# Scaled queries written once and spread over two head tiles by small transfers

## The chip, the cores and the metric

One core of a Trainium2 chip runs the whole kernel. The metric is the device time of one execution in microseconds (us). The kernel before takes 842.66 us, the median of three runs (841.91 to 842.76).

## The reference

Two independent parts are computed and laid side by side in the output (1 x 2048 x 1024). Part A is multi-head attention over 2048 tokens with 32 heads of 16 features; part B is a long causal convolution.

```
def _A_ref(x, wqkv, wo):                 # x 1x2048x512, H = 32, Dh = 16
    qkv = (x @ wqkv).reshape(B, S, 3, H, Dh) ...
    scores = einsum("bhqd,bhkd->bhqk", q, k) * (Dh ** -0.5)
    p = softmax(scores, axis=-1)
    o = einsum("bhqk,bhkd->bhqd", p, v)
    return o.transpose(...).reshape(B, S, D) @ wo

def _B_ref(q, k, v, shift_k, ssm_k, ssm_D):
    k_shift = four-tap causal filter of k with shift_k
    kv = k_shift * v
    y = causal convolution of kv with ssm_k (2048 taps, by FFT) + kv * ssm_D
    return q * y
```

## The kernel before

**Attention.** The 32 heads stand in four groups ("octets") of eight, so that eight heads of 16 features fill the 128 partitions. The queries stand in four blocks of 512. That gives 16 pairs (octet, query block), numbered p in `PAIRS` (L350), and each pair has two groups n = 2p and 2p+1: four of its eight heads are the even ones, four the odd ones. One group is 16 key tiles of 128 keys by 4 heads, 64 blocks, so there are 32 x 64 = 2048 blocks in all. A block is one matmul of 32 contraction rows (L670): its keys are 32 partitions of `KTo`, holding two neighbouring heads, its queries are 32 partitions of `QT`. So that only one of the two heads counts, the `QT` tile of parity par (0 for even heads, 1 for odd) must be zero in the 16 rows of the other head. `QT` has three slots of two such tiles (`R_Q` = 3), slot p % 3 for pair p.

The score blocks land in PSUM banks 0 to 5. ScalarE (ACT) takes two or three adjacent banks in one exponential (`emit_exp`, L703) and writes them to `PT`. Some blocks are given to VectorE (DVE) instead (`exp_on_dve`, L739 to 763): five DVE instructions per block, one that reads the bank into `FX` (L745), three steps of a polynomial in `EH` (L752) and one that writes `PTD` (L757). TensorE (PE) then multiplies the exponentials by the values (`emit_pv`, L786, bank 6), the DVE divides by the sums (`finish_group`, L847 to 867), and the output projection follows (L897, L905).

**Queries.** A projection unit ("q", p) is four matmuls (L390) into one bank. `evac_unit` (L433) then takes it out in two DVE passes (L440). Each reads the whole bank, multiplies by a column of `MASK` and writes a whole `QT` tile; `MASK` holds the scale in the rows of one parity and 0 in the rows of the other. Pair 0 has passes of its own (L541).

**Convolution.** Rows of the reversed filter are loaded from a scratch in device memory into four slots of `WR`, 128 "quads" of four 512 KB transfers, issued on SP's queue (`load_wr`, L932). They are multiplied on PE in steps of four small matmuls (`conv_lags`, L956, bank 7), 8192 in all.

**Order of work.** Every instruction is recorded by a planner in Python that keeps an estimated clock for each engine (`Eng.op`, `dma`) and fixes the program order of each engine before the program is built; on the chip, the engines wait for each other by semaphores alone. The main loop (L1183) goes over T, one round for each ACT exponential: `emit_qk` gives out banks and score matmuls, `pv_step` the value matmuls, `emit_bg` background work (projection units by their due rounds in `jobs`, L1007, and convolution steps), `warm_up` (L1161) fills PE's remaining time with matmuls of zeros. DVE work is put in place by `urgent` (L287) and `advance` (L277). The constants at the top (L38 to L97) set margins, window lengths and the convolution's pace. POOL's queue carries a few memsets, the loads and stores of `QN`, the load of the output weights and the output stores (L908). A unit ("q", p) is due eight rounds before its pair's first round and can be placed once pair p - 3 has had its last score matmul.

Of the kernel before, what the change touches and what calls it, by code (L numbers as in the profile page):

```python
# [15 lines left out]
QB = 512  # L16
# [20 lines left out]
N_OPEN = 68  # L37
LAGS = 8  # L38
PACE = 1.0
KEYS0 = 256  # L40
# [20 lines left out]
SLOT = 16  # L61
OPEN = 70
CLOSE = 10
REST = 2
LEN = 4
WIN_D = 2
S_U = 0.4
S_FX = 0.45
# [3 lines left out]
JOIN = 0.05  # L72
JOIN2 = 0.1
MOST = 3
LOOK = 8
GAP = 8
# [4 lines left out]
BACKLOG = 5.8  # L81
MARGIN = 0.3
SPARE = 0
# [12 lines left out]
WAIT = 1.5  # L96
LATE = 0.1  # L97
V512 = (0.60, 0.726)
# [68 lines left out]
def bass_concat_heads__mha_block__ssm_conv_h3__prompt_kernel(  # L167
# [21 lines left out]
    def sem(name):  # L189
        return enter(nc.semaphore(name))  # L190

    def sb(name, shape, dt=BF16):
        return enter(nc.sbuf_tensor(name, shape, dt))
# [4 lines left out]
    QT = sb("QT", [128, R_Q, 2, QB])  # L198
    VA = sb("VA", [128, 2, KT, VROW])
    PT = sb("PT", [128, R_PT, QB])  # L200
    WR = sb("WR", [128, R_W, S])
# [93 lines left out]
    d_q = [DmaSem(sem(f"d_q{i}")) for i in range(2)]  # L295
    d_outB = [DmaSem(sem(f"d_outB{i}")) for i in range(2)]
    d_outE = DmaSem(sem("d_outE"))
    d_outA = [DmaSem(sem(f"d_outA{i}")) for i in range(R_A)]
# [45 lines left out]
    pool.op(lambda e: e.memset(VA[:, :, :, 0:8 * VW].rearrange("p s k (h e) -> p (s k) h e", e=VW)[:, :, :, DH:VW], 1.0))  # L344
    h_va1 = pool.op(lambda e: e.memset(VA[:, :, :, 8 * VW:VROW].rearrange("p s k e -> p (s k) e"), 1.0))
    h_kz0 = pool.op(lambda e: e.memset(KZS[:, :, S:S + PAD], 0.0))
    act.op(lambda e: e.activation(JNK[:, 1:2], JNK[:, 0:1], ACT.Exp), [h_j], inc=False)
# [85 lines left out]
    def evac_unit(u, bank, h):  # L433
        kind = u[0]
        if kind == "q":
            p = u[1]
            last = [qk_done[2 * (p - R_Q) + i] for i in range(2)] if p >= R_Q else []
            for par in range(2):
                hh = urgent(
                    lambda e, par=par: e.tensor_scalar(QT[:, p % R_Q, par, :], PS[:, bank, :], MASK[:, par:par + 1], None, ALU.mult),  # L440
                    [h, h_mask] + last, us=(0.658, 0.784))
                h_q[2 * p + par] = hh
        elif kind == "k":
# [560 lines left out]
    def step(n):  # L1004
        return PLAN * n // (NQB * NG)

    jobs = [(step(2 * p) - 8, ("q", p)) for p in range(2, 16)]  # L1007
    jobs += [(step(OF.index(o)) - 16 + 4 * sc, (x, o, sc)) for o in (2, 3) for sc in range(4) for x in "kv"]
# [250 lines left out]
```

## Time and profile before

| | us |
|---|---|
| median of three timed runs | 842.66 (841.91 to 842.76) |
| the profiled execution, its own time | 845.53 |
| its span, first to last instruction | 843.8 |
| ACT busy | 828.5 (98%) |
| DVE busy | 812.1 (96%) |
| PE busy | 788.0 (93%) |
| POOL busy | 17.6 (2%) |

The span is the time from the first to the last instruction of the profiled execution; 1.7 us of its own time lie outside. Matmuls overlap on PE, so its busy share is no measure of how near its peak it runs. In a row of a group, the numbers after the first bar are the time in which at least one instruction of the group ran and the mean duration of one, in nanoseconds; after the second bar stands the idle time of the engine just before them and what ended it. Instructions of ACT and DVE overlap their neighbours at the ends, so that the mean duration is larger than the distance from start to start.

### The profile page before, as it was taken

How to read it: one execution, taken by the hardware profiler on the slowest of the kernel's cores; microseconds unless marked ns; L12 is line 12 of the kernel's file. 1: busy time of each engine (PE TensorE's matmuls, PEld its weight loads, DVE VectorE, ACT ScalarE, POOL GpSimd, SP SyncE). 2: the span in 40 equal slices, each digit the busy share in tenths (PEclk: the TensorE clock that was granted, in tenths of full speed). 3: DMA queues.
4: the chain of work that ended last, by engine and by line, in shares of the span. 5: the costliest groups of instructions: out<-in, count | busy, mean ns of one | idle time of the engine just before them, and what ended most of it. 6: DMA issues, size and time to landing. Idle time of an engine off the chain costs nothing.

```text
span 843.8 us, 30582 instructions
## 1 busy us (share of the span) xinstructions
PE 788.0 (93%) x13766; PEld 334.9 (40%) x13808; DVE 812.1 (96%) x1382; ACT 828.5 (98%) x727; POOL 17.6 (2%) x34
## 2 busy tenths in 40 slices
PE   8898999999999999999999999999999999999897
PEld 3343334443433334344434434344443434343342
DVE  4999999999999999999999999999999999999895
ACT  6999999999999999999999999999999999999897
POOL 2000000000000000000000100000000000010000
PEclk9999999999999999999999999999999999999899
DMA  9996199999999999989999999999999999999942
GB/s 227 262 297 245 48 406 386 359 385 366 395 354 395 350 376 332 348 270 342 404 380 388 384 391 380 369 408 398 405 408 350 378 407 410 403 347 360 354 181 75
DMA packets 105394, 289.44 MB, mean 343 GB/s; under 512 B 35760, under 2 KB 37808, under 8 KB 104880
## 3 DMA queue, kind: packets, MB, share of 16 engines
q1 hardware_dynamic: 102256, 280.80, 90.3%
q0 software_dynamic: 1808, 6.29, 2.2%
q8 instruction: 109, 1.79, 0.8%
q10 hardware_dynamic: 1200, 0.39, 0.2%
q14 instruction: 21, 0.17, 0.1%
HBM read 276.83 MB, written 6.42 MB: 336 GB/s over the span
## 4 chain that ended last, share of the span: by engine, by line
ACT 95%; PE 3%; SPq 1%; DMA 1%; issue 0%; DVE 0%
ACT PT L703 94%; PE PS L670 1%; SPq L257 1%; DMA xT<-in_A_x_dram 1%; PE PS L956 1%; PE PS L786 1%; PE PS L897 0%; DVE DT L847 0%; ACT QT L915 0%; PE PS L1161 0%; DVE FX L745 0%; PE PS L399 0%; PE PS L981 0%; PE PS L422 0%; DVE DTN L858 0%
## 5 line engine op out<-in xcount | busy, mean ns | idle before, releaser
L703 ACT ACTIVATE PT<-PS 128x1536 bf16<-128x1536 f32 (+2 forms) x722 | 825.5, 1455 | 4.1 <-PE PS L670 3.7
L670 PE MATMUL PS<-QT,KTo 32*128 32x512 bf16 x2048 | 285.8, 385 | 34.7 <-ACT PT L703 8.3
L752 DVE SCALAR_TENSOR_TENSOR EH<-EH,FX 128x512 f32<-128x512 f32 x446 | 295.3, 678 | 0.2
L956 PE MATMUL PS<-WR,KV 128*16 128x128 bf16 (+15 forms) x8192 | 218.9, 220 | 2.6 <-issue 2.6
L786 PE MATMUL PS<-PT,VA 128*32 128x512 bf16 x1825 | 197.9, 390 | 2.0 <-DVE DT L847 1.1
L956 PEld LDWEIGHTS PS<-WR,KV 128*14 128x14 bf16 (+15 forms) x8192 | 146.8, 87 | 88.9 <-issue 53.7
L1161 PE MATMUL PS<-IDN,ZW 128*32 128x512 bf16 (+4 forms) x666 | 168.5, 335 | 0.9 <-DVE DT L847 0.6
L670 PEld LDWEIGHTS PS<-QT,KTo 32*128 32x128 bf16 x2048 | 72.5, 91 | 230.9 <-ACT PT L703 180.1
L745 DVE TENSOR_SCALAR FX<-PS 128x512 f32<-128x512 f32 x223 | 151.8, 682 | 5.3 <-PE PS L670 4.5
L752 DVE SCALAR_TENSOR_TENSOR EH<-FX 128x512 f32<-128x512 uint16 x223 | 150.6, 681 | 0.1
L757 DVE SCALAR_TENSOR_TENSOR PTD<-EH,FX 128x512 uint16<-128x512 f32 x223 | 150.3, 676 | 0.1
L786 PEld LDWEIGHTS PS<-PT,VA 128*32 128x32 bf16 x1825 | 47.6, 93 | 108.0 <-issue 95.0
L786 PE MATMUL PS<-PTD,VA 128*32 128x512 bf16 x223 | 69.4, 384 | 0.0
L1161 PEld LDWEIGHTS PS<-IDN,ZW 128*32 128x32 bf16 (+1 forms) x666 | 54.4, 96 | 25.4 <-issue 6.3
L847 DVE STREAM_TRANSPOSE DT<-PS 128x512 f32<-128x512 f32 x32 | 22.7, 709 | 8.4 <-PE PS L786 7.8
L970 DVE CAST YB<-PS 128x512 bf16<-128x512 f32 x32 | 21.8, 681 | 1.0 <-PE PS L956 0.5
L440 DVE TENSOR_SCALAR QT<-PS,MASK 128x512 bf16<-128x512 f32 x30 | 20.9, 737 | 0.6 <-PE PS L390 0.3
L422 PE MATMUL PS<-WKV,xT 128*128 128x128 bf16 x256 | 19.0, 220 | 0.4 <-DVE KTo L446 0.2
L399 PE MATMUL PS<-xT,WKV 128*128 128x512 bf16 (+1 forms) x50 | 15.1, 373 | 3.8 <-issue 1.6
L897 PE MATMUL PS<-WKV,OTN 128*128 128x512 bf16 x51 | 16.4, 383 | 2.2 <-issue 1.6
L786 PEld LDWEIGHTS PS<-PTD,VA 128*32 128x32 bf16 x223 | 17.1, 95 | 0.7
L422 PEld LDWEIGHTS PS<-WKV,xT 128*128 128x128 bf16 x256 | 14.4, 98 | 6.6 <-issue 4.3
(61 smaller groups left out, 197.8 us busy)
## 6 DMA issues: line engine op xcount, KB each, us to landing
WR<-kz_scratch SPq DMA_DIRECT2D x512, 512.0 KB, 7.3
kz_scratch<-WR SPq DMA_DIRECT2D x1, 2176.0 KB, 9.1
QN<-in_B_q_dram POOLq DMA_DIRECT2D x2, 1024.0 KB, 12.1
out_dram<-QN POOLq DMA_DIRECT2D x2, 1024.0 KB, 8.2
out_dram<-OUTA POOLq DMA_DIRECT2D x12, 128.0 KB, 5.9
QN<-in_B_ssm_k_dram SPq DMA_DIRECT2D x1, 1024.0 KB, 8.2
OTN<-in_B_ssm_k_dram SPq DMA_DIRECT2D x1, 1024.0 KB, 9.0
WR<-in_B_v_dram SPq DMA_DIRECT2D x2, 512.0 KB, 12.5
```

The costliest lines, as they stand in the source:

```text
L422: ins = e.matmul(PS[:, bank, 128 * j:128 * j + 128], lhsT=xT[:, dc, (4 * sc + j) * 128:(4 * sc + j + 1) * 128], rhs=WV[:, dc, o * 128:(o + ...
L440: lambda e, par=par: e.tensor_scalar(QT[:, p % R_Q, par, :], PS[:, bank, :], MASK[:, par:par + 1], None, ALU.mult),
L670: ins = e.matmul(PS[:, bank, :], lhsT=KTo[32 * s:32 * s + 32, OF[n_] % 2, kt * 128:(kt + 1) * 128], rhs=QT[32 * s:32 * s + 32, n_ // 2 % R ...
L703: h_exp[T] = act.op(lambda e: e.activation(PT[:, p0:p0 + n, :].rearrange("p b f -> p (b f)"), PS[:, banks[0]:banks[0] + n, :].rearrange("p ...
L745: h_f = urgent(lambda e: e.tensor_scalar(fx, PS[:, bank, :], FIX_ADD, FIX_HI, ALU.add, ALU.min), [h, h_last.get(i - R_FX)], slack=S_FX)
L752: st["h"] = dve.op(lambda e: e.scalar_tensor_tensor(eh, src, (A3, A2, A1)[j], frac, ALU.add, ALU.mult), [st["h"], h_last.get(i - R_EH)], u ...
L757: lambda e: e.scalar_tensor_tensor(out16, eh, A4, fx, ALU.mult, ALU.add),
L786: ins = e.matmul(dst, lhsT=w, rhs=rhs, start=(k == 0), stop=(k == KT - 1), tile_position=(0, 32 * s))
L847: h_t = urgent(lambda e: e.transpose(out=dt, in_=PS[:, PVB, :]), [h, h_mul.get(n - 1)], slack=S_T, us=(0.63, 0.751))
L956: ins = e.matmul(PS[32 * c:32 * c + NB - n, BGB, 128 * (kk % 4):128 * (kk % 4) + 128], lhsT=KV[:, qd, n:NB, c], rhs=WR[:, r + c, 128 * (NB ...
L970: hh = urgent(lambda e: e.tensor_copy(YB[:, half, :].rearrange("p (k i) -> p k i", k=4), src), [h, h_yb[0]], slack=S_C, us=V512)
L1161: pe.op(lambda e, s=s, k=k, rhs=rhs, bank=bank, rows=rows, c0=c0, first=first: e.matmul(PS[32 * s:32 * s + rows, bank, c0:c0 + 128 * k], l ...
```

## The change

A new tile `QS` takes the scaled queries in one DVE pass that reads the bank once. Eight transfers on POOL's queue, each of 16 partitions by 512 elements (16 KB), copy the rows of the even heads to tile 0 of the pair's `QT` slot and the rows of the odd heads to tile 1. The other rows of slots 1 and 2 are set to zero once at the start by POOL; slot 0 has them from pair 0's masked passes. The pass into `QS` waits for the transfers of the pair before, the transfers wait for the last score matmul of the pair that had the slot, and the score matmuls wait for the transfers in place of a DVE pass. A query unit is due 24 rounds before its pair instead of 8. Nine constants of the planner change too, and with them the order of all engines' work.

```diff
-LAGS = 8
-PACE = 1.0
+LAGS = 6
+PACE = 1.05
-OPEN = 70
+OPEN = 80
-REST = 2
-LEN = 4
+REST = 3
+LEN = 3
-S_U = 0.4
+S_U = 0.5
-JOIN2 = 0.1
+JOIN2 = 0.15
+Q_DUE = 24
-MARGIN = 0.3
+MARGIN = 0.35
-LATE = 0.1
+LATE = 0.2
...
+    QS = sb("QS", [128, QB])
...
+    d_qs = [[DmaSem(sem(f"d_qs{i}{par}")) for par in range(2)] for i in range(2)]
...
+    h_qt0 = pool.op(lambda e: e.memset(QT[:, 1:R_Q, :, :].rearrange("p r n f -> p (r n f)"), 0.0), us=(1.5, 1.6))
...
             last = [qk_done[2 * (p - R_Q) + i] for i in range(2)] if p >= R_Q else []
+            hh = urgent(lambda e: e.tensor_scalar(QS[:, :], PS[:, bank, :], QSCALE, None, ALU.mult),
+                        [h] + [h_q[2 * (p - 1) + i] if p > 1 else None for i in range(2)], us=V512)
             for par in range(2):
-                hh = urgent(
-                    lambda e, par=par: e.tensor_scalar(QT[:, p % R_Q, par, :], PS[:, bank, :], MASK[:, par:par + 1], None, ALU.mult),
-                    [h, h_mask] + last, us=(0.658, 0.784))
-                h_q[2 * p + par] = hh
+                for r0 in range(16 * par, 128, 32):
+                    h_q[2 * p + par] = dma(pool, d_qs[p % 2][par], QT[r0:r0 + 16, p % R_Q, par, :], QS[r0:r0 + 16, :],
+                                           [hh, h_qt0] + last, kb=16)
...
-    jobs = [(step(2 * p) - 8, ("q", p)) for p in range(2, 16)]
+    jobs = [(step(2 * p) - Q_DUE, ("q", p)) for p in range(2, 16)]
```

## Prediction

> **What bounds the kernel now.** I read the page's busy table first, then the chain of work that ended last, then the groups of ACT by shape, then the two waits that ACT has.
>
> ```profile
> span 843.8 us, 30582 instructions
> PE 788.0 (93%) x13766; PEld 334.9 (40%) x13808; DVE 812.1 (96%) x1382; ACT 828.5 (98%) x727; POOL 17.6 (2%) x34
> ...
> ACT 95%; PE 3%; SPq 1%; DMA 1%; issue 0%; DVE 0%
> ...
> L703 ACT ACTIVATE PT<-PS 128x1536 bf16<-128x1536 f32 (+2 forms) x722 | 825.5, 1455 | 4.1 <-PE PS L670 3.7
> ...
> 13.73 508.06 ACT PT L703 x446
> ...
> 836.78 0.41 PE PS L786 x2
> ```
>
> The end is set by one engine: 95% of the chain is ACT, and its 722 exponentials fill 825.5 us with 4.1 us of idle time before them. In the chain ACT sets the pace from 13.73 us, the first stretch without a break, to 836.78, where the tail begins. So the time is the number and size of ACT's exponentials plus its holes plus head and tail. DVE at 96% matters because each score block that it takes is one that ACT need not take. The price of an exponential comes from its shapes:
>
> ```profile
> L703 ACT ACTIVATE PT<-PS 128x1536 bf16<-128x1536 f32 x375 | 580.4, 1662 | 1.2 <-PE PS L670 1.0
> L703 ACT ACTIVATE PT<-PS 128x1024 bf16<-128x1024 f32 x344 | 394.7, 1227 | 1.8 <-PE PS L670 1.7
> L703 ACT ACTIVATE PT<-PS 128x2048 bf16<-128x2048 f32 x3 | 5.6, 1877 | 1.1 <-PE PS L670 1.0
> ```
>
> A third block makes one 1662 - 1227 = 435 ns longer, a third and fourth together 650 ns. The mean durations overlap their neighbours, so the distance b of a two-block exponential follows from the busy time: 722 b + 375 x 0.435 + 3 x 0.650 = 825.5, b = 0.915 us; a three-block one costs 1.350 us, and the mean is 825.5 / 722 = 1.143 us. ACT's only large hole in mid-run is here:
>
> ```profile
> 785.01 0.37 PE L956 MATMUL PS<-WR,KV 128*2 128x128 bf16 x5 [2.08 <-issue]
> 786.51 2.54 ACT L703 ACTIVATE PT<-PS 128x1024 bf16<-128x1024 f32 x2 [1.70 <-PE PS L670]
> 789.62 1.45 ACT L703 ACTIVATE PT<-PS 128x1536 bf16<-128x1536 f32 x1 [0.57 <-PE PS L670]
> 791.49 2.36 ACT L703 ACTIVATE PT<-PS 128x1536 bf16<-128x1536 f32 x2 [0.42 <-PE PS L670]
> ...
> 784.00:792.00 8.00, 6.66 (x93) 2.64 (x93) 5.01 (x10) 5.25 (x5) 0.00 (x0) 0.57 1.02 380
> ```
>
> PE stood still for 2.08 us inside a run of matmuls, released by nothing the profile shows; its granted clock was 0.57 in the stretch 784 to 792, and ACT lost 1.70 + 0.57 + 0.42 = 2.69 us. The profiled execution took 845.53 us; without this hole it is 842.84, and the median of the timed runs is 842.66. I take it that the timed runs have no such hole, so the sum is applied to 842.66; against the profiled execution the same sum is subtracted from 845.53.
>
> **The change, part by part.** The counts are those of the built order of both kernels; the durations are rows of the profile.
>
> *DVE.* Thirty masked passes go, fifteen plain ones come.
>
> ```profile
> L440 DVE TENSOR_SCALAR QT<-PS,MASK 128x512 bf16<-128x512 f32 x30 | 20.9, 737 | 0.6 <-PE PS L390 0.3
> L745 DVE TENSOR_SCALAR FX<-PS 128x512 f32<-128x512 f32 x223 | 151.8, 682 | 5.3 <-PE PS L670 4.5
> ...
> 93.15 1.41 DVE L440 TENSOR_SCALAR QT<-PS,MASK 128x512 bf16<-128x512 f32 x2
> 94.55 0.69 DVE L745 TENSOR_SCALAR FX<-PS 128x512 f32<-128x512 f32 x1
> ...
> sum 600.00, PE 568.34 PEld 244.63 DVE 595.07 ACT 599.90 POOL 6.35; mean PE 94.72 PEld 40.77 DVE 99.18 ACT 99.98 POOL 1.06
> ```
>
> Two masked passes hold DVE from 93.15 to 94.55, 1.40 us. The plain pass has the form of the pass into FX (PSUM in, one constant, 512 columns), which has 682 ns and, as the rows further down show, starts 0.60 us after its neighbour. That frees 15 x (1.40 - 0.60) = 12.0 us. The new order spends it: 228 blocks on DVE instead of 223, five instructions each, 5 x 5 x 0.60 = 15.0 us. DVE is thus 3 us fuller, on an engine that is busy 595.07 of 600 us in the six stretches from 100 to 700; this is where a lateness would come from.
>
> *ACT.* 372 exponentials of three blocks (375 before), 346 of two (344), 3 of four (3): 1820 blocks for 1825. The sum is -3 x 1.350 + 2 x 0.915 = **-2.22 us**. All of it lies on the path. The head (up to 13.7 us) and the tail (seven two-block exponentials, the last projections, the last stores) have the same work, so they cost nothing new.
>
> *PE.* The score, value, projection and convolution matmuls are the same 2048, 2048 and so on (five value matmuls read PTD instead of PT). What fills its gaps shrinks, 632 filler matmuls for 666; that filler is the cover of every shift in the order:
>
> ```profile
> L1161 PE MATMUL PS<-IDN,ZW 128*32 128x512 bf16 (+4 forms) x666 | 168.5, 335 | 0.9 <-DVE DT L847 0.6
> ```
>
> 168.5 us of PE is stuffing, so I cost the changed constants at nothing. If the cover is gone at one place, the price is of the kind of the hole above, 1.70 us for a 2.08 us standstill and 2.69 with what follows.
>
> *POOL and its transfers.* 120 transfers of 16 x 1 KB and a clearing of 128 x 2048 come. The clearing stands before the filter's padding, early; POOL clears 128 x 512 in 568 ns, four times that is 2.3 us, and POOL idles 11.6 us before its next work (rows below). In the queue the copies stand ahead of the padding memsets, two loads of QN, the load of the weights and the output stores; POOL is busy 17.6 us in all, and every copy's slot was released earlier than its pass, so nothing is held long. The cost of a copy has no row. Nearest:
>
> ```profile
> L257 POOL DMA_DIRECT2D out_dram<-OUTA x12 | 6.5, 544 | 227.2 <-DVE OUTA L905 227.2
> L257 POOL DMA_DIRECT2D QN<-in_B_q_dram x2 | 2.5, 1236 | 33.3 <-PE PS L411 23.7 <-DMA out_dram<-QN 9.5
> L257 POOL DMA_DIRECT2D out_dram<-QN x2 | 2.3, 1160 | 480.5 <-DVE QN L990 480.5
> L502 POOL TENSOR_SCALAR_AFFINE_SELECT OTN<-SHK 128x2048 bf16<-128x2048 bf16 x1 | 2.0, 2012 | 11.6 <-DMA SHK<-in_B_shift_k_dram 11.6
> L344 POOL MEMSET VA<- 128x512 bf16 x1 | 0.6, 568 | 0.0
> ...
> L257 ACTq DMA_DIRECT2D out_dram<-QT x1: 373/373/373, 840.8 to 840.8; - x1
> DMA to landing us min/median/max: 2.2/2.2/2.5
> ...
> DMA to landing us min/median/max: 5.1/5.9/7.1
> ```
>
> The first landing line is that of the last stores (QT, 2.2 us), the second that of the output tiles (OUTA, 5.1 to 7.1 us). Issuing costs between 0.37 us (ACT's queue) and 1.24 us (a whole 1 MB load on POOL); landing between 2.2 and 7.1 us. I take the OUTA row, 0.544 and 5.9 us: same queue, rows of 1 KB, the smallest count of rows.
>
> *The two new waits.* (1) The score matmuls wait for the copies. From the unit to the first use the order leaves 48 or more exponentials (55 us), except 18 for pair 1 and 10 for pair 2. For pair 2 that is 10 x 1.143 = 11.4 us; needed are 0.9 us of matmuls, 0.68 of the pass, three issues and a landing for the even heads: 0.9 + 0.68 + 3 x 0.544 + 5.9 = 9.1 us. It fits; with the upper ends (3.7 and 7.1) it takes 12.4 and ACT loses 1.0 us. (2) The pass into QS waits for all eight copies of the pair before, and DVE takes its work in order: every FX, EH and PTD behind it waits too, and the PSUM banks that FX frees, which the score matmuls need. Two places are near: pair 3 behind pair 2, and pair 10 behind pair 9. Between pass 2 and pass 3 stand 13 DVE instructions, so pass 3 comes up 14 x 0.60 = 8.4 us after pass 2; the copies need 0.68 + 7 x 0.544 + 5.9 = 10.4 us, so DVE would stand 2.0 us. But ACT feels it only at a score matmul: the one that needs pass 2's bank stands behind exponential 70, the one that needs pass 3's bank behind exponential 79, 9 x 1.143 = 10.3 us later, with about half an exponential in hand while ACT works on the next. 10.4 against 10.3 to 10.9: nothing. Lower end (0.37, 2.2): 5.5 us, nothing either. Upper end (1.24, 7.1): 0.68 + 8.68 + 7.1 = 16.5 us, ACT loses up to 6.2. Pair 10 has 12 exponentials, 13.7 us: nothing at the taken value, up to 2.8 at the upper end. I take 0, near the OUTA row, and keep +10 us (1.0 + 6.2 + 2.8) as the far end.
>
> Here a rule speaks against the change. POOL's transfer and DVE side by side in this trace:
>
> ```profile
> 465.45 0.68 DVE L757 SCALAR_TENSOR_TENSOR PTD<-EH,FX 128x512 uint16<-128x512 f32 x1
> 466.05 1.29 DVE L752 SCALAR_TENSOR_TENSOR EH<-FX 128x512 f32<-128x512 uint16 x2
> 467.25 0.68 DVE L752 SCALAR_TENSOR_TENSOR EH<-EH,FX 128x512 f32<-128x512 f32 x1
> ...
> 465.85 1.15 POOL L257 DMA_DIRECT2D out_dram<-QN  x1 [404.87 <-DVE QN L990]
> ```
>
> DVE keeps its 0.60 us from start to start (466.05 to 467.25 for two) while POOL issues from 465.85 to 467.00, and POOL's 1.15 us is the mean of its two such stores (1160 ns above). The Trainium skill's page "SBUF — State Buffer", section "SBUF: two separate sides", says that a transfer issued on POOL's queue has its descriptors written by POOL and that a DVE instruction in a two-port mode locks POOL out until it ends. By that rule each of the eight issues could wait out one DVE instruction, an estimated 0.68 + 0.544 = 1.22 us, and the eight copies would make it 840.4 + 4.8 + 1.4 = 846.6 by the waits (2) above. These rows do not agree with it for the instructions that fill DVE here, as neither engine is slowed.
>
> *Bytes.* 120 x 16 KB = 1.97 MB come to the 289.44 MB, 0.7%. The filter rows are the heavy user:
>
> ```profile
> 500.00:600.00 100.00, 94.93 (x1801) 40.80 (x1802) 99.29 (x170) 99.97 (x89) 0.77 (x1) 1.00 1.02 391
> ...
> GB/s 227 262 297 245 48 406 386 359 385 366 395 354 395 350 376 332 348 270 342 404 380 388 384 391 380 369 408 398 405 408 350 378 407 410 403 347 360 354 181 75
> DMA packets 105394, 289.44 MB, mean 343 GB/s; under 512 B 35760, under 2 KB 37808, under 8 KB 104880
> ```
>
> The new order asks for 1400 convolution matmuls between exponentials 150 and 250 (1312 before): 21.9 quads of 2.097 MB in 114 us, 402 GB/s, against 410 reached in a slice. Four slots of filter rows lie ahead of it. I cost it at nothing.
>
> **Sum.** -2.22 + 0 + 0: 842.66 - 2.2 = 840.4; the profiled execution 845.53 - 2.2 = 843.3 if the hole at 785 stays, 840.6 if not. Small unevenness of a new order (0.1) gives **840.5**.
>
> **The rivals.**
>
> *The pass waits for its own copies (the other side).* One mechanism, at pass 3: if the copies take longer than 10.3 us, ACT loses the excess. Each 0.1 us on the issue is 0.7 us on the chain. The time passes 844.35 (slower) when the chain passes 14.0 us (3.7 lost here, 0.3 at pair 10), an issue of 1.06 us with 5.9 landing. At the upper end, 840.4 + 10.0 = 850.4; at 1.24 and 5.9, chain 15.3, 5.0 lost there and 1.6 at pair 10: 847.0. For it: no two POOL transfers stand back to back in this trace, so what eight in a row cost is not shown. Against it: 0.544 is for 128 rows, here are 16. The other rule goes further: the Trainium skill's page "DMA: Bandwidth & Descriptors", section "Anatomy of one DMA — SWDGE (gpsimd) path", gives 2.0 us plus bytes over 436 GB/s for one such transfer; by it the chain would be an estimated 6.5 us and no wait would stand at all, while the OUTA row measures 5.9.
>
> *The new order opens holes.* DVE 3 us fuller, the convolution denser between exponentials 150 and 250, a PE standstill in the timed runs. Price: one or two holes of 1.7 to 2.7 us, 842.1 to 845.8. For it: DVE has 5 us of idle time in 600. Against it: outside the hole at 785 the order before had 4.1 - 2.69 = 1.4 us of them.
>
> *The change does not do what it says.* The passes go but the planner does not turn them into blocks on DVE: excluded, the built order has 228. That the copies' cost returns as idle time of DVE alone would leave 840.4, since ACT's count is fixed.
>
> **How the numbers follow.** About 0.2% (1.7 us: below 840.97, above 844.35) can be told from no change. Forecast (840.0 to 840.97): 0.58, all faster. Pass waiting: 0.20 (0.03 of it by POOL being held up by DVE), of which 0.02 still faster, 0.09 the same, 0.09 slower. Holes: 0.22, 0.02 faster, 0.12 the same, 0.08 slower. Together faster 0.62, same 0.21, slower 0.17. The range runs from 839.9 to 845.8: it takes in the forecast, all of the holes' prices and the nearer half of the waiting, and leaves out the far end.
>
> **What would show it.** In the changed kernel's profile: 721 exponentials in about 823.3 us of busy time (right if within 0.5); the passes into QS at 0.68 us; DVE busy near 815 us; POOL's copies near 0.54 us each and landings below 6 us; no wait of ACT near exponential 79 (pair 3) or near exponential 363 (pair 10). Wrong if copies take over 1 us each or land after 7 us, if DVE shows an idle time of over 2 us before the third pass into QS and ACT a hole behind it, or if ACT's idle time before its exponentials is above 4 us.

## The result, and the profile after

The changed kernel takes 841.51 us (median of 22 runs, 840.02 to 844.72), the kernel before 844.10 us in the 22 runs beside it (841.91 to 848.49). The ratio is 0.9972, with a 95% interval of 0.9959 to 0.9984: 2.4 us faster, 1.4 to 3.5. That is the forecast side; the forecast size was -2.2 us. The profiled execution took 842.58 us; before it was 845.53.

The page of the changed kernel, with its busy table, its chain and its first group:

```profile
span 840.8 us, 30758 instructions
PE 792.8 (94%) x13774; PEld 333.3 (40%) x13774; DVE 814.7 (97%) x1392; ACT 825.8 (98%) x726; POOL 77.6 (9%) x155
...
ACT 92%; PE 3%; DVE 3%; DMA 1%; issue 0%
...
L708 ACT ACTIVATE PT<-PS 128x1536 bf16<-128x1536 f32 (+2 forms) x721 | 822.9, 1455 | 2.6 <-PE PS L675 2.6
```

The same kernel's groups by shape, those of ACT, POOL and DVE that the prediction priced:

```profile
L708 ACT ACTIVATE PT<-PS 128x1536 bf16<-128x1536 f32 x372 | 575.2, 1663 | 0.7 <-PE PS L675 0.7
L708 ACT ACTIVATE PT<-PS 128x1024 bf16<-128x1024 f32 x346 | 395.4, 1229 | 0.4 <-PE PS L675 0.4
...
L259 POOL DMA_DIRECT2D QT<-QS x120 | 58.7, 497 | 481.5 <-DVE QS L442 165.7 <-DVE DR L859 105.7 <-PE PS L961 86.2
...
L349 POOL MEMSET QT<- 128x2048 bf16 x1 | 1.8, 1794 | 0.0
...
L442 DVE TENSOR_SCALAR QS<-PS 128x512 bf16<-128x512 f32 x15 | 10.2, 682 | 0.4 <-PE PS L394 0.4
```

ACT still sets the end. Its exponentials fall from 825.5 to 822.9 us and the idle time before them from 4.1 to 2.6 us; together 4.1 us. Not all of the idle time is alike: before, 2.69 us of it were the hole at 785 and 1.04 us the wait of the first exponential; now 1.50 us are that first wait. The small holes in mid-run thus grew, from 0.4 to 1.1 us. The span falls by 3.0 us only, because the head of this execution was longer: ACT waited 4.46 us for its first keys in place of 3.44, and the first exponential started at 9.67 us in place of 8.18. The head varies by about 1 us between executions of one kernel (the rest in the table below, 17.1 and 16.2 us for the changed kernel), so this is not laid to the change. The prices of a shape stayed (1663 for 1662 ns, 1229 for 1227); only the counts moved. POOL's 58.7 us of copies are on no path.

The two waits that were to decide are at pairs 2 and 3. The timeline of the changed kernel around them, DVE first, then POOL's copies, then SP's first filter loads; each row has start, duration, what ran, and in brackets the engine's idle time before it with its releaser:

```profile
93.29 0.70 DVE L442 TENSOR_SCALAR QS<-PS 128x512 bf16<-128x512 f32 x1
...
101.10 0.70 DVE L762 SCALAR_TENSOR_TENSOR PTD<-EH,FX 128x512 uint16<-128x512 f32 x1
101.70 0.70 DVE L442 TENSOR_SCALAR QS<-PS 128x512 bf16<-128x512 f32 x1
...
94.28 3.83 POOL L259 DMA_DIRECT2D QT<-QS  x8 [27.69 <-DVE QS L442]
102.69 3.81 POOL L259 DMA_DIRECT2D QT<-QS  x8 [4.58 <-DVE QS L442]
...
100.64 1.88 SPq L259 DMA_DIRECT2D WR<-kz_scratch  x4
```

The pass of pair 3 comes 8.41 us after that of pair 2 and has no bracket: DVE did not stand. What the copies themselves took, from the view of the tile QS in three stretches of the changed kernel (pair 2, pair 3, pair 9), each with the issues and the time from issue to landing (shortest, median, longest):

```profile
L259 POOL DMA_DIRECT2D QT<-QS x8: 484/484/501, 94.3 to 97.6; - x8
...
DMA to landing us min/median/max: 1.6/1.6/1.6
...
L259 POOL DMA_DIRECT2D QT<-QS x8: 484/484/487, 102.7 to 106.0; - x8
...
DMA to landing us min/median/max: 5.2/5.4/5.9
...
L259 POOL DMA_DIRECT2D QT<-QS x8: 484/484/487, 414.0 to 417.3; - x8
...
DMA to landing us min/median/max: 2.0/5.4/5.8
```

Pair 2's last copy starts its issue at 97.6 and lands 1.6 us later, at 99.2, before SP issues the first filter loads at 100.64. So its chain, from the start of the pass, is 6.0 us where 10.4 was taken. Pair 3's copies run beside the filter stream and need 5.2 to 5.9 us. The other near place has less room: pass 10 comes 12.4 us after pass 9, and the copies of pair 9 take 10.0 us of that here and 11.5 in a second profile of this kernel (after_again below). The windows of the same kernel show the two traffics (the last column is GB/s, the one before it the busy share of the DMA engines, the third from the end PE's granted clock):

```profile
94.00:99.00 5.00, 4.59 (x64) 1.57 (x65) 5.00 (x9) 5.00 (x5) 3.83 (x8) 1.00 0.10 26
99.00:110.00 11.00, 10.39 (x222) 4.34 (x221) 11.00 (x19) 11.00 (x12) 3.81 (x8) 1.00 0.78 243
...
100.00:700.00 600.00, 573.05 (x10678) 243.79 (x10676) 595.09 (x1013) 598.87 (x531) 56.22 (x113) 1.00 1.01 376
```

From 100 to 700 DVE is busy 595.09 us, as before (595.07): the freed time was spent on the five blocks. POOL is at 56.22 us instead of 6.35, and DVE keeps its 0.60 us from start to start while POOL issues: it makes fourteen steps from 93.29 to 101.70. POOL's eight issues fill 3.83 us at 0.48 us each, so neither engine held the other up.

### The profile page after: what moved, and what is told of

The parts are those of the page before. It is cut to its first block, busy times and chain, and to the rows that moved or that the text cites. A ratio compares the mean times of both kernels' runs of the same rounds, so it can differ in the third digit from the quotient of the medians.

```text
span 840.8 us, 30758 instructions
## 1 busy us (share of the span) xinstructions
PE 792.8 (94%) x13774; PEld 333.3 (40%) x13774; DVE 814.7 (97%) x1392; ACT 825.8 (98%) x726; POOL 77.6 (9%) x155
## 4 chain that ended last, share of the span: by engine, by line
ACT 92%; PE 3%; DVE 3%; DMA 1%; issue 0%
ACT PT L708 92%; DVE EH L757 2%; PE PS L675 1%; PE PS L791 1%; DMA xT<-in_A_x_dram 1%; PE PS L961 1%; DVE PTD L762 1%; DVE FX L750 1%; PE PS L536 0%; PE PS L415 0%; PE PS L1166 0%; DVE DT L852 0%; ACT QT L920 0%; DVE DTN L863 0%; PE PS L902 0%
## 5 line engine op out<-in xcount | busy, mean ns | idle before, releaser
L708 ACT ACTIVATE PT<-PS 128x1536 bf16<-128x1536 f32 (+2 forms) x721 | 822.9, 1455 | 2.6 <-PE PS L675 2.6
L757 DVE SCALAR_TENSOR_TENSOR EH<-EH,FX 128x512 f32<-128x512 f32 x456 | 305.1, 687 | 0.0
L961 PE MATMUL PS<-WR,KV 128*15 128x128 bf16 (+15 forms) x8192 | 213.4, 219 | 1.1 <-issue 1.1
L961 PEld LDWEIGHTS PS<-WR,KV 128*1 128x1 bf16 (+15 forms) x8192 | 144.7, 87 | 82.3 <-issue 47.1
L1166 PE MATMUL PS<-IDN,ZW 128*32 128x512 bf16 (+4 forms) x632 | 162.4, 335 | 0.2
L750 DVE TENSOR_SCALAR FX<-PS 128x512 f32<-128x512 f32 x228 | 156.9, 690 | 2.4 <-PE PS L675 1.3
L762 DVE SCALAR_TENSOR_TENSOR PTD<-EH,FX 128x512 uint16<-128x512 f32 x228 | 155.7, 685 | 0.0
L757 DVE SCALAR_TENSOR_TENSOR EH<-FX 128x512 f32<-128x512 uint16 x228 | 155.7, 689 | 0.0
L259 POOL DMA_DIRECT2D QT<-QS x120 | 58.7, 497 | 481.5 <-DVE QS L442 165.7
L403 PE MATMUL PS<-xT,WKV 128*128 128x512 bf16 (+1 forms) x64 | 18.1, 377 | 0.6 <-DVE KTo L451 0.5
L394 PE MATMUL PS<-xT,WQ 128*128 128x512 bf16 x60 | 17.6, 384 | 0.2 <-DVE VA L473 0.2
```

The costliest lines, as they stand in the source:

```text
L259: f(outp, inp).then_inc(dsem.sem, 16)
L708: h_exp[T] = act.op(lambda e: e.activation(PT[:, p0:p0 + n, :].rearrange("p b f -> p (b f)"), PS[:, banks[0]:banks[0] + n, :].rearrange("p ...
L750: h_f = urgent(lambda e: e.tensor_scalar(fx, PS[:, bank, :], FIX_ADD, FIX_HI, ALU.add, ALU.min), [h, h_last.get(i - R_FX)], slack=S_FX)
L757: st["h"] = dve.op(lambda e: e.scalar_tensor_tensor(eh, src, (A3, A2, A1)[j], frac, ALU.add, ALU.mult), [st["h"], h_last.get(i - R_EH)], u ...
L762: lambda e: e.scalar_tensor_tensor(out16, eh, A4, fx, ALU.mult, ALU.add),
L961: ins = e.matmul(PS[32 * c:32 * c + NB - n, BGB, 128 * (kk % 4):128 * (kk % 4) + 128], lhsT=KV[:, qd, n:NB, c], rhs=WR[:, r + c, 128 * (NB ...
```

## The experiments

The theory: the gain is the number of score blocks that DVE takes over, and the copies cost nothing because they land before anything needs them. Rivals: the gain comes from the new constants alone, which give an order with fewer holes; or the waits of the copies cost something and the constants pay for it. All ratios are to the kernel before, run on the same chip beside it (its medians were 843.49, 843.42 and 843.98 us in the three sets). For each profiled execution the time splits into three parts: the busy time of ACT's exponentials, ACT's idle time before them (holes, with the first exponential's own wait of 1 to 2 us among them), and all the rest, worked out as the difference.

| kernel | ratio (95%) | profiled, us | exponentials | holes | rest |
|---|---|---|---|---|---|
| before | 1 | 845.53 | 825.5 | 4.1 | 15.9 |
| changed | 0.9972 (0.9959 to 0.9984) | 842.58 | 822.9 | 2.6 | 17.1 |
| cap223 | 1.0007 (0.9996 to 1.0018) | 844.13 | 825.2 | 2.5 | 16.4 |
| copies_only | 1.0015 (1.0000 to 1.0029) | 843.23 | 823.9 | 3.3 | 16.0 |
| consts_only | 1.0026 (1.0012 to 1.0040) | 845.10 | 825.1 | 4.4 | 15.6 |
| copies_only2 | 1.0028 (1.0012 to 1.0044) | 846.48 | 823.9 | 5.6 | 17.0 |
| after_again | 0.9982 (0.9968 to 0.9996) | 841.58 | 823.0 | 2.4 | 16.2 |
| margin_only | 0.9976 (0.9962 to 0.9990) | 844.02 | 823.7 | 3.6 | 16.7 |
| copies_x2 | 1.0101 (1.0074 to 1.0127) | 850.27 | 823.9 | 10.4 | 16.0 |
| copies_x3 | 1.0260 (1.0234 to 1.0285) | 867.94 | 824.7 | 26.8 | 16.4 |
| x3_two | 1.0036 (1.0015 to 1.0056) | 846.67 | 823.6 | 7.3 | 15.8 |
| two_same | 0.9998 (0.9976 to 1.0019) | 841.36 | 822.6 | 1.8 | 17.0 |
| due8 | 1.0010 (0.9988 to 1.0032) | 842.87 | 823.9 | 2.9 | 16.1 |
| two_tiles_fit | 0.9996 (0.9976 to 1.0017) | 843.53 | 823.1 | 4.5 | 15.9 |

A profiled execution is one draw from runs that spread by 3 to 10 us, so the ratios decide and the split tells where to look.

**Are the five blocks the gain?** cap223 is the changed kernel with DVE stopped at 223 blocks, as many as before.

```diff
+        if i >= 223:
+            return None
```

> The changed kernel, with at most 223 blocks given to DVE, as many as before; copies, constants and waits unchanged. Built order: 341 two-block, 377 three-block, 3 four-block exponentials. Theory: -3 x 0.915 + 2 x 1.350 = 0.0 us against the kernel before in ACT's work, exponentials busy about 825.5 us, so 2.2 us slower than the changed kernel, with DVE idle some 12 us more near the end. Rival (the shorter query path itself is worth the gain, not the five blocks): it stays at ratio 0.997.

Its groups by shape, ACT's two large ones:

```profile
L708 ACT ACTIVATE PT<-PS 128x1536 bf16<-128x1536 f32 x377 | 580.0, 1668 | 1.3 <-PE PS L675 1.2
L708 ACT ACTIVATE PT<-PS 128x1024 bf16<-128x1024 f32 x341 | 388.9, 1231 | 0.0
```

Five three-block exponentials more and five two-block ones less; the exponentials take 825.2 us and the whole gain is gone (1.0007). Five blocks are worth 2.3 us of exponentials by the two profiles; the ratios differ by 0.35%, 2.9 us (0.25% against the second set of the changed kernel, after_again). The freed DVE time alone brings nothing: DVE fell to 799.3 us and now stands up to 12.9 us waiting for PE.

**Copies or constants?** Four runs: the copies with the nine old constants, twice (copies_only, copies_only2); the nine new constants with the old masked passes (consts_only); the changed kernel once more (after_again).

```diff
 copies_only, copies_only2 (from the changed kernel)
-LAGS = 6
-PACE = 1.05
-OPEN = 80
-REST = 3
-LEN = 3
-S_U = 0.5
-JOIN2 = 0.15
-MARGIN = 0.35
-LATE = 0.2
+LAGS = 8
+PACE = 1.0
+OPEN = 70
+REST = 2
+LEN = 4
+S_U = 0.4
+JOIN2 = 0.1
+MARGIN = 0.3
+LATE = 0.1
 consts_only (from the kernel before): the same nine the other way round
```

> The copies and the due round 24, with the nine planner constants of the kernel before. Built order: 343 two-block, 374 three-block, 3 four-block and 1 one-block exponentials, 227 blocks on DVE. Theory (the gain is ACT's count, paid by the DVE time that the masked passes held): against the kernel before -0.915 - 1.350 + 0.480 = -1.8 us, ratio 0.998, exponentials busy about 823.7 us. Rival (the gain is in the new constants, the copies bring nothing): ratio 1.000. Rival (the copies cost transfer time that the constants had hidden): above 1.000, with holes before ACT's exponentials of over 3 us in the profile.

> The nine new constants alone, masked passes and due round 8 kept. Built order: 356 two-block, 366 three-block, 3 four-block, 1 one-block exponentials, 225 blocks on DVE. Theory: 12 x 0.915 - 9 x 1.350 + 0.480 = -0.7 us against the kernel before, ratio 0.999, exponentials busy about 824.8 us, DVE fuller than before because it still makes thirty masked passes. Rival (the constants bring the gain): -2.3 us, ratio 0.997, and the profile has less than 1.5 us of holes before the exponentials.

Neither half gains; both are slower. The exponentials came as their counts say: 823.9 us for copies_only (374 of three blocks, 227 blocks on DVE), 825.1 us for consts_only (366 of three blocks but 356 of two, 225 on DVE). What spoils them, as far as the profiles show, are holes. The largest of copies_only, in its timeline:

```profile
551.15 0.68 DVE L750 TENSOR_SCALAR FX<-PS 128x512 f32<-128x512 f32 x1
551.75 0.70 DVE L852 STREAM_TRANSPOSE DT<-PS 128x512 f32<-128x512 f32 x1
552.38 0.65 DVE L975 CAST YB<-PS 128x512 bf16<-128x512 f32 x1
...
553.09 0.62 PE L986 MATMUL PS<-IDN,YB 128*128 128x128 bf16 x8 [1.10 <-DVE YB L975]
...
554.08 3.71 ACT L708 ACTIVATE PT<-PS 128x1536 bf16<-128x1536 f32 x3 [0.70 <-PE PS L675]
```

The pass into YB, which takes a finished convolution bank out, stands behind two other DVE passes; PE waits 1.10 us for it with score matmuls queued behind, and ACT 0.70 us for those. No copy has a part in it. The ratio above 1 and the 3.3 us of holes are also what the rival with hidden transfer costs had said; against it, neither DVE nor a matmul waits for a copy anywhere in this profile. Is such a hole chance or order?

> The copies with the nine old constants once more. Its first runs gave 1.0015 where ACT's count said 0.998. Theory (the order itself has holes): the holes of its first profile come back at the same exponentials, the one of 0.8 us at 478 above all, where PE waited 1.1 us for the pass into YB behind a queue of DVE passes; ratio 1.001. Rival (chance standstills of PE filled its first runs): other places, ratio near 0.998.

> The changed kernel once more, on the chip of the next three, as their measure and for a second profile. Theory: ratio to the kernel before 0.997; exponentials busy about 822.9 us; the small holes near 219, 393 and 618 us return at the same exponentials (181, 334, 533), since they belong to the order, while standstills of PE that the profile ascribes to nothing may come elsewhere. Rival (the first ratio was luck of the runs; the two-tile kernel with the same order gave 0.9998): ratio 0.999 to 1.000.

In copies_only2 the holes came back at the same places: exponentials 138, 150, 355, 478, 513, 602, 642, 713 and 717 in both runs (lost there, by the distance between ends of exponentials: 0.20 and 1.57, 0.15 and 0.16, 0.16 and 0.16, 0.81 and 1.25, 0.37 and 0.37, 0.49 and 0.49, 0.28 and 0.28, 0.16 and 0.16, 0.16 and 0.16 us). In the changed kernel the holes at exponentials 334 (393 us) and 351 (412 us) came back (0.40, then 0.72; 0.50, then 0.79), those at 181 and 533 (0.31, 0.34) did not. So most holes belong to the order that the constants give. Chance comes on top; the 1.57 us at exponential 138 of copies_only2 has this in its timeline:

```profile
169.20 0.22 PE L961 MATMUL PS<-WR,KV 128*16 128x128 bf16 x2
171.11 0.40 PE L961 MATMUL PS<-WR,KV 128*16 128x128 bf16 x14 [1.70 <-issue]
...
171.89 1.45 ACT L708 ACTIVATE PT<-PS 128x1536 bf16<-128x1536 f32 x1 [1.46 <-PE PS L675]
```

That is a standstill of the kind at 785 in the kernel before: inside a run of matmuls, released by nothing that the profile shows. In copies_only the same place lost 0.20 us.

The traces say more about these standstills than the timeline does. Their DMA view has a queue of its own for instructions; in the changed kernel it moves 109 blocks of 16 KB, one about every 7 us:

```profile
q8 instruction: 109, 1.79, 0.9%
```

In the fourteen profiles PE stands for 0.4 us or more without a releaser 22 times after the first 20 us, and every time it goes on 2.25 to 2.70 us after such a block began to move; a moment taken at random lies in that stretch in 7% of cases. PE passes about 250 matmuls and weight loads from one block to the next, so the blocks are most likely its own instructions, and it stands because they come late. No run here changes them, so this is not shown by an experiment. The place then belongs to the order and only the length is chance: the matmul before exponential 351 stands 0.60 us in the changed kernel, 0.89 in after_again, 1.41 in x3_two, 2.29 in copies_x3, and under 0.1 us in two_same, cap223 and copies_x2.

**One constant.** margin_only is copies_only with one of the nine new constants, a margin of the planner.

```diff
-MARGIN = 0.3
+MARGIN = 0.35
```

> The copies with one of the nine constants changed, MARGIN 0.35, the spare time that the planner leaves ACT before background work on PE. Built order: 338 two-block, 378 three-block, 3 four-block exponentials, 226 blocks on DVE. Theory (a constant matters by the order that falls out, here one with fewer holes): -6 x 0.915 + 3 x 1.350 = -1.4 us, ratio 0.998, holes between the exponentials below 2 us in the profile. Rival (all nine together make the gain): ratio 1.001 as with the old constants.

0.9976, as good as all nine (0.9972 and 0.9982). Its order has 378 exponentials of three blocks and 338 of two, 823.7 us, only 0.2 less than copies_only; but of the nine holes none is left, and three of 0.15 to 0.21 us in other places are all that it has in mid-run. Its profiled run is the longest of its times (median 842.25), with a slow start: ACT stood 1.33 us before its second exponential and 0.44 before its third, where the changed kernel runs on without a break. The mid-run holes of over 0.1 us add up to 2.8 us in copies_only, 1.6 and 1.8 us in the two profiles of the changed kernel, and 0.5 us in margin_only. With the exponentials that puts copies_only some 2 us behind the changed kernel, where the ratios say 2.8 to 3.6 us; the rest is not explained. So the copies gain with either set of constants that leaves few holes, and lose with the old set that leaves nine.

**How near is the wait?** copies_x2 and copies_x3 cut each copy into two (8 + 8 rows) or three (6 + 5 + 5), with the order of all other instructions unchanged.

```diff
+            for a, b in zip(cuts, cuts[1:]):
+                f(outp[a:b, :], inp[a:b, :]).then_inc(dsem.sem, 16)
...
-                                           [hh, h_qt0] + last, kb=16)
+                                           [hh, h_qt0] + last, kb=16, cuts=[0, 8, 16])
 copies_x3: cuts=[0, 6, 11, 16]
```

> The changed kernel with each copy cut into two of 8 rows: 240 transfers, same bytes, same order on every engine. In the changed kernel's trace pass 2 starts at 93.29, its last copy lands at 99.25 (5.96 us) and pass 3 starts at 101.70; pair 9's copies land 10.0 us after its pass. Eight more issues at 0.477 us from start to start add 3.8 us: 9.8 and 13.8 us. Theory (ACT feels the wait of the pass only beyond 10.3 us for pair 3 and 13.7 us for pair 10): DVE stands about 1.4 us before pass 3 and 1.8 us before pass 10, ACT loses about 0.1 us, ratio as the changed kernel's, 0.997. Rival (DVE's standing is lost time): about 3 us slower than the changed kernel, ratio 1.001. Rival (the number of transfers costs in itself, by contention with the filter rows): holes before exponentials away from pairs 3 and 10.

copies_x2 around pair 3, its timeline on DVE and ACT:

```profile
91.74 0.68 DVE L447 TENSOR_SCALAR QS<-PS 128x512 bf16<-128x512 f32 x1
...
99.55 0.68 DVE L767 SCALAR_TENSOR_TENSOR PTD<-EH,FX 128x512 uint16<-128x512 f32 x1
106.80 0.69 DVE L447 TENSOR_SCALAR QS<-PS 128x512 bf16<-128x512 f32 x1 [6.57 <-DMA QT<-QS]
...
108.29 1.02 ACT L713 ACTIVATE PT<-PS 128x1024 bf16<-128x1024 f32 x1 [5.48 <-PE PS L680]
109.68 2.54 ACT L713 ACTIVATE PT<-PS 128x1536 bf16<-128x1536 f32 x2 [0.36 <-PE PS L680]
```

Its sixteen copies of pair 2 in the view of the tile:

```profile
L262 POOL DMA_DIRECT2D QT<-QS x16: 512/518/521, 92.7 to 100.3; - x16
...
DMA to landing us min/median/max: 1.6/1.8/6.3
```

And the window behind the hole, with PE's clock third from the end:

```profile
106.00:114.00 8.00, 6.36 (x99) 2.54 (x101) 7.09 (x12) 4.82 (x4) 6.22 (x13) 0.64 0.54 171
```

The rival of the prediction is real. Issuing costs the same for 8 rows as for 16, so twice the copies fill twice the time: (100.3 - 92.7) / 15 = 0.51 us each. But the chain grew from 6.0 to 15.1 us (91.74 to 106.80), 5 us more than the issues explain, and the ratio, 1.0101, is above both recorded ones. SP issues the first filter loads at 99.07 in this run, 7.3 us after the pass; the copies that are still on the way then land up to 6.3 us after their issue, not 1.6. DVE stood for 6.57 us, and 5.48 of them reached ACT. I had taken a chain of up to 10.3 us to be free; here ACT's first hole is smaller than DVE's wait by 1.1 us only, and 0.36 us more follows while PE's granted clock is 0.64.

> The changed kernel with each copy cut into three (6, 5 and 5 rows): 360 transfers, same bytes, same order. Sixteen more issues at 0.477 us add 7.6 us to the chain from pass to last landing: 13.6 us for pair 2, 17.6 for pair 9, 17.8 for pair 3. Theory (ACT loses what exceeds 10.3 us before pass 3, 13.7 before pass 10, 17.1 before pass 4): DVE stands about 5.2 us before pass 3, ACT loses 3.3 + 3.9 + 0.7 = 7.9 us, 848 us where the changed kernel has 840 to 841.5, ratio to before 1.006. Rival (copies are off the path): ratio 0.997. Rival (all of DVE's standing is lost): 5.2 + 5.6 + 3.1 = 13.9 us, ratio 1.014.

copies_x3 at the same place, its timeline:

```profile
111.59 0.69 DVE L447 TENSOR_SCALAR QS<-PS 128x512 bf16<-128x512 f32 x1 [8.82 <-DMA QT<-QS]
...
113.08 1.02 ACT L713 ACTIVATE PT<-PS 128x1024 bf16<-128x1024 f32 x1 [7.72 <-PE PS L680]
```

8.82 and 7.72: again 1.1 us in hand and the rest handed on. The price is steep: over the whole kernel DVE waits 17.8 us for copies in three places, and the time is 2.6% above before, more than any theory had. To see that it is this wait and not the transfers, x3_two keeps the 360 copies and the order but writes pairs in turn into two QS tiles, so that a pass waits for the copies of the pair before the last.

```diff
+    QS2 = sb("QS", [128, 2, QB])
...
+            QS = QS2[:, p % 2, :]
...
+            waits = [w for w in waits if w[0] is pe.sem] + [h_q[2 * (p - 2) + i] for i in range(2) if p > 2]
```

> As the one before, but with two tiles QS used in turn, so a pass waits for the copies of the pair before last; the order of every engine is that of the changed kernel. Theory (the loss is the pass's wait, not the transfers): no standing of DVE before a pass, and the score matmuls of pair 2 still in time (the even heads' copies land near 101.2 us, needed near 103): ratio 0.997, as the changed kernel. Rival (360 transfers on POOL's queue cost by themselves, in transfer engines or POOL): the loss of the three-fold copies stays, ratio 1.006.

The pass into QS waits for no copy any more and the ratio falls from 1.0260 to 1.0036: 2.2 of the 2.9 percentage points that the cut copies cost were that wait (of 2.6, counted from two_same on the same chip). What is left shows in two places of its timeline, POOL, PE and ACT:

```profile
30.46 13.54 POOL L262 DMA_DIRECT2D QT<-QS  x24 [12.86 <-DVE QS L448]
43.98 0.14 POOL L339 MEMSET QN<- 128x32 bf16 x1
44.04 0.18 POOL L339 MEMSET OTN<- 128x16 bf16 x2
...
44.27 0.61 PE L420 MATMUL PS<-OTN,QN 128*128 128x128 bf16 x8 [2.33 <-POOL OTN L339]
...
45.25 1.02 ACT L717 ACTIVATE PT<-PS 128x1024 bf16<-128x1024 f32 x1 [1.82 <-PE PS L684]
...
413.71 0.40 PE L800 MATMUL PS<-PT,VA 128*32 128x512 bf16 x4 [1.41 <-issue]
```

Two small memsets of the filter's padding stand on POOL behind 24 copies; PE needs the padding and waits 2.33 us. It is the queue that the prediction named and costed at nothing. The other is the standstill before exponential 351. In the changed kernel the eight copies end at 36.40, and the memset of OTN starts at 37.70 after a wait for DVE, so the copies do not hold it:

```profile
31.21 5.20 POOL L259 DMA_DIRECT2D QT<-QS  x8 [14.32 <-DVE QS L442]
36.40 0.14 POOL L334 MEMSET QN<- 128x32 bf16 x1
37.70 0.16 POOL L334 MEMSET OTN<- 128x16 bf16 x2 [1.16 <-DVE WR L494]
```

**Would more room help?** two_same is the changed kernel with the two QS tiles and the same order; due8 makes the unit due 8 rounds ahead, as before, in place of 24.

```diff
 two_same: QS2 and the waits as in x3_two, without the cuts
 due8:
-Q_DUE = 24
+Q_DUE = 8
```

> The changed kernel with two tiles QS used in turn, same order on every engine. Theory: the copies already land before the next pass needs the tile (5.96 of 8.4 us, 10.0 of 12), so nothing changes: ratio 0.997, DVE's idle time as in the changed kernel. Rival (the single tile costs in the timed runs, where landings vary up to 7.9 us): faster than the changed kernel by 1 us or more, ratio 0.996.

> The changed kernel with query units due 8 rounds ahead, as before the change. Built order: 348 two-block, 371 three-block, 3 four-block exponentials, 227 blocks on DVE. Theory: units come later but most have tens of exponentials of room; ACT's work is -2.22 + 2 x 0.915 - 1.350 = -1.7 us against the kernel before; holes appear only where a score matmul comes less than about 10 us after its pair's pass, under load (5.2 us median landing plus 3.8 of issues plus 1). Between -1.7 and +3 us, ratio 0.998 to 1.004. Rival (the due round does not matter): ratio 0.998 and no new wait of score matmuls for QT.

two_same is level with before (0.9976 to 1.0019) by its median, though its fastest run, 841.26 us, and its profile, the lowest of all, are near the changed kernel's. Its interval still holds the 0.9982 of after_again, which has the same order. A second tile brings nothing that these runs can tell, as there was no wait to take away. It was near, though: in this profile the copies of pair 9 landed 12.8 us after their pass, 0.4 us after pass 10 came up.

due8 has 348 + 371 + 3 exponentials, 823.9 us as counted (823.8), and 1.0010 (0.9988 to 1.0032): the gain is lost. Its largest hole is the rival of the prediction, with whole copies. From its timeline, DVE, PE and ACT:

```profile
420.69 0.69 DVE L442 TENSOR_SCALAR QS<-PS 128x512 bf16<-128x512 f32 x1
431.00 0.69 DVE L442 TENSOR_SCALAR QS<-PS 128x512 bf16<-128x512 f32 x1 [1.96 <-DMA QT<-QS]
...
431.84 0.39 PE L675 MATMUL PS<-QT,KTo 32*128 32x512 bf16 x3 [1.50 <-DVE QS L442]
...
432.27 1.02 ACT L708 ACTIVATE PT<-PS 128x1024 bf16<-128x1024 f32 x1 [1.04 <-PE PS L675]
```

Pass 10 comes up 8.35 us after pass 9, the copies of pair 9 run under the filter stream and land after 10.2 us, so DVE stands for 1.96 us and ACT for 1.04. Two smaller holes follow up to 454 us, of 0.17 and 0.41 us; the second is released by a late pass into YB, not by copies. With another due time the planner also makes another order, so this does not price the due time by itself.

**A version to beat both.** two_tiles_fit has two tiles with the shorter waits known to the planner, and thirteen constants chosen for the most blocks on DVE, 230.

```diff
-T_DVE = 6
-CLOSE = 10
-REST = 3
-LEN = 3
...
-BACKLOG = 5.8
-LATE = 0.2
+T_DVE = 4
+CLOSE = 8
+REST = 2
+LEN = 5
...
+BACKLOG = 5.4
+LATE = 0.15
 and S_FX 0.45 to 0.55, S_T 0.2 to 0.3, S_C 0.3 to 0.4, PLAN 710 to 715,
 JOIN 0.05 to 0.08, JOIN2 0.15 to 0.2, GAP 8 to 10
```

> A version meant to beat both: two tiles QS in turn, each pass waiting for the copies of the pair before last, and thirteen constants set anew for an order with 230 blocks on DVE: 347 two-block, 372 three-block, 2 four-block exponentials. Theory: 3 x 0.915 - 3 x 1.350 - 1.565 = -2.9 us against the kernel before, ratio 0.9966, 0.7 us ahead of the changed kernel, exponentials busy about 822.3 us. Rival (DVE, 6 us fuller than in the changed kernel, is late and opens holes): no faster than the changed kernel, holes above 2 us released by DVE passes.

It does not beat it. The view of PE's waits in this kernel, in all, times, longest:

```profile
PE PS L792 <- DVE DT L853: 7.0, 14, 0.8
```

DVE is busy 819.7 us, PE waits 7.0 us in fourteen places for DVE's passes (0.6 us in two places in the changed kernel), and ACT's idle time is 4.5 us, in some dozen small holes. The two blocks more came back as holes.

## Why the prediction was right, and where it was off

**ACT's sum** (-2.22 us): right. The built order has 721 exponentials in the shapes forecast; 822.9 us of busy time against 823.3. The price from shapes, 0.915 us for two blocks and 0.435 us for a third, gave 825.5 for cap223 (825.2 measured) and 823.7 for copies_only (823.9); it held within 0.7 us in every kernel but copies_x3 (823.3, measured 824.7). That the count is what the gain hangs on is shown by cap223. The measured gain is 2.4 us with an interval of 1.4 to 3.5, too wide to tell it from 2.2, and two more terms stand in it, which nearly cancel (last two points below).

**DVE**: right. Pass 682 ns (682 taken), 814.7 us busy (815), 8.41 us from pass 2 to pass 3 (8.4), and no wait.

**The copies' issue and landing**: the issue was 0.48 us (0.544 taken; in pair 1, the first, one of the eight took 1.33). The landing was taken as one number, 5.9 us from the store of OUTA. It has two values: 1.6 us for pair 2, and 5.2 to 5.9 for pair 3 under the filter stream. So at the place where I looked for the danger there was more room than I worked out: the copies were there 2.5 us before the pass came up, and a further 1.1 us would not have reached ACT. The prediction did not ask when the filter stream begins; that it began 1.4 us after pair 2's last landing (99.25, 100.64) was luck. One of its own signs of being wrong came up without harm: two of the 120 landings took over 7 us (7.1 at pair 4, 7.9 at pair 5), where the next pass was 63 and 38 us away. The Trainium skill's page "DMA: Bandwidth & Descriptors", section "Anatomy of one DMA — SWDGE (gpsimd) path", with its 2.0 us plus bytes, was near for pair 2 (an estimated 2.04 us for 16 KB against 1.6) and far off for pair 3 (5.4 us). Neither row nor page alone had both.

**The rival of the waiting pass**: it did not occur, but its shape was wrong too. I had it grow by 0.7 us for each 0.1 us of issue. In fact it jumps: as soon as the last copies are issued into the filter stream, some 7.3 us after the pass, the landing grows by 4 to 5 us at once. Twice the copies cost 1.3 percentage points, three times 2.9. And the slack was smaller than taken: 1.1 us between DVE's wait and ACT's, in both runs (0.9 in due8), not the 10.3 - 8.4 = 1.9 of the count of exponentials. So "nothing" did not follow from the taken chain: 10.4 - 8.4 - 1.1 is 0.9 us lost, and due8 lost 1.04 us with a chain of 10.2 us at pair 10.

**POOL held up by DVE**: it was not, as weighed. Issues stay 0.48 us apart and DVE's instructions 0.60 with both at work, so the locking that the Trainium skill's page "SBUF — State Buffer", section "SBUF: two separate sides", describes does not show for the DVE instructions that stand there.

**The changed constants at nothing**: this is the step whose reason failed. I argued that 168.5 us of filler covers every shift. Filler covers PE's time, but not a wait of PE in program order for a DVE pass that comes late. With the copies and the old constants the kernel is 0.15 to 0.28% slower than before; with one constant changed 0.24% faster. For the full change the holes stayed below the 4 us that I had set as the bound (2.6 us). But in mid-run they grew by 0.7 us and more where I had put 0.1, and that there were no larger ones was luck of that order as far as my argument went. The rival "the new order opens holes" deserved more than its 0.22: copies_only and two_tiles_fit have holes in which no copy has a part, and due8 has such holes beside the one of its copies.

**The point from which the sum was made**: I took the timed runs to have no standstill, since 845.53 less the hole at 785 was 842.84, near the 842.66 of three runs. Over 22 runs the median before is 844.10. The absolute forecast of 840.5 was thus 1.0 us low, with the right difference. Long standstills without a releaser were in the profiles of the kernel before (2.08 us), copies_only2 (1.70), x3_two (1.41) and copies_x3 (2.29); behind all but that of copies_only2 the granted clock was 0.57 over the next 4 to 8 us. Every timed run comes with its mean granted clock: in the three sets beside the experiments it is below 0.9985 in 42 of 93 runs of the kernel before, whose medians are 1.2 to 2.4 us above those of the others, and in none of the 33 runs of the changed kernel. So nearly half of the timed runs before did have such holes, as far as the clock tells, and the changed kernel escapes them. Beside after_again, the changed kernel is ahead of all 35 runs before by 1.75 us on the average, and of the 19 at full clock by 1.3 us (0.3 to 2.2). The measured 2.4 us is thus the count's 2.2, less about 1 us of small holes of the new order, plus what the old order loses by standstills; that the sum came so near the forecast is in part luck. One execution of each kernel is profiled, so the standstills in the timed runs are argued from the clock and not seen.

Still open: a test that PE waits for its instructions in such a standstill, why the changed kernel escapes the long ones, and how eight of the nine constants act singly; only MARGIN was tried alone.

## What to carry to other kernels

Where one engine sets the pace with instructions of known price, count them: their busy time followed the count within 0.7 us in all kernels here but the one with the longest waits. The whole time followed it only where the order left few holes. Price a small transfer by what else its DMA queues carry at that moment, and ask when the heavy stream begins: a chain with 3.5 us to spare (8.4 + 1.1 - 6.0) cost ACT 5.5 us when twice the issues stretched it into the stream. When a change comes together with a new order of the program, run the parts apart before crediting one of them; here neither half gained alone, and one scheduling constant made the difference.

## What the runs showed of the hardware that was not expected

- A 16 KB copy between SBUF tiles on POOL's queue lands 1.6 us after its issue with the DMA engines nearly idle (0.10 busy share), and 5.2 to 5.9 us under the filter stream; over all 120 copies 1.6 to 7.9 us, median 5.2.
- POOL issues such copies 0.48 to 0.51 us apart whether they have 16, 8 or 5 rows, so cutting a transfer in two doubles its price in issue time. In the first pair single issues took up to 1.33 us.
- PE can stand 0.4 to 2.3 us inside a run of matmuls with no releaser in the trace; all 22 such standstills ended 2.25 to 2.70 us after a 16 KB block began to move on the instruction queue. Behind the one at 785 in the kernel before the granted clock was 0.57 for 8 us; behind DVE's long wait in copies_x2 it was 0.64 in the 8 us that followed, so a hole can cost more than its own length. It need not: behind standstills of 1.70 us (copies_only2), 1.39 (cap223) and 1.32 (two_tiles_fit) the granted clock was 1.00 in the next 4 us.
